# Softmax and feature steps of the first chunk moved between ScalarE, VectorE and GpSimd in a fused attention and feed-forward kernel

## The chip, the cores and the metric

The kernel runs on one core of a Trainium2 chip. A core has five engines that each work through their own queue in order: PE (TensorE, matmuls), DVE (VectorE), ACT (ScalarE), POOL (GpSimd) and SP, which here only issues DMAs. They wait for each other through semaphores. The metric is the device time of one execution in microseconds; lower is better. The kernel before took 885.22 us in the median of three runs (881.85 to 885.75).

## What is computed

The reference is attention with sparse masks on 8 sequences of 576 positions, 8 heads of width 64, followed by a feed-forward layer on the 4608 tokens:

```python
scores = scale * np.matmul(q, k.transpose(0, 1, 3, 2))
rel = pos[:, None] - pos[None, :]
mask_local = (rel >= 0) & (rel < stride)                        # heads 0 to 3, stride 32
mask_strided = (rel >= 0) & (pos[None, :] % stride == pos[:, None] % stride)   # heads 4 to 7
scores = np.where(masks, scores, -1e9)
attn = np.exp(scores - max); attn = attn / (sum + 1e-9)
x = matmul(attn, v) regrouped to (4608, 512)
h = np.maximum(x @ w_in, 0.0)          # w_in: 512 x 2048
out = h * h @ w_out                    # w_out: 2048 x 512
```

All of it is in fp32 accuracy: on PE each fp32 operand of the feed-forward layer is split into a high and a low part, and a product is three matmuls (high by high, low by high, high by low).

## The kernel before, in words

The 4608 tokens go in 12 chunks of 384. A chunk first needs its attention output x (written xlh, xll for the local heads and xsh, xsl for the strided heads, high and low part). Then `up` (L452) makes for each of 16 slices j of the hidden width twelve 128x384 matmuls into one of three PSUM banks (h), squares the positive part and splits it into gh and gl. `down` (L480) multiplies gh and gl by a slice of w_out, nine 128x512 matmuls, into three accumulator banks (y). While PE does the ups and downs of one chunk, the other engines make the attention of the next one.

The first chunk has nothing to hide behind, so all its heads run on PE in pairs (`pe_pair`, L292): `first` are the two pairs of local heads, `late` the two pairs of strided ones. A pair has these steps: scores on PE (L319); mask and minimum on DVE (L324); exponentials with their sum on ACT, one instruction per block (L345, `single`, the local pairs), or a subtraction on POOL (L347), one exponential per head on ACT (L348) and a sum on DVE (L349) (the others); the reciprocal of the sum on DVE (L350, L351); the division on POOL (L353), in SBUF; a transpose on PE (L359) and a copy out of PSUM on ACT (L360); the product with v on PE (L367, L378); high part on ACT (L382) and low part on DVE (L383).

Beside it `convert` (L147) unpacks the weights, which arrive as 1 MB tiles of 64-bit floats, in halves of 512: one scaling of the tile on ACT (L154), then for each half a step on ACT into PSUM (z, L166), one on DVE (L169), the high part on ACT (L172) and the low part on POOL (L173). `behind(..)` lets such work be issued only after a named instruction. In the prologue (L588 to L627) the order in which `next(..)` steps the pairs and the weights is the order in which they are handed to the scheduler, which then places each engine's queue; in the first chunk each up and down (L632 to L636) hands in two weight halves, behind the gh of that step (L652, L653), and a share of the next chunk's heads (L661 to L681). `zeros` (L583) issues matmuls on zeros whose result nobody reads: 60 at the start, 30 after the scores of the local pairs and 30 after those of the first strided pair.

In the first chunk `up` squares with ACT and DVE (L470, L471: ACT writes relu(h) to SBUF, DVE multiplies it with max(h, 0) in PSUM), ACT writes gh (L475) and DVE gl (L476); in the others ACT does both (L473, L474).

Of the kernel before, what the change touches and what calls it, by code (L numbers as in the profile page):

```python
# [22 lines left out]
P = 128  # L23
# [63 lines left out]
def attn_moe(ctx: ExitStack, tc, qk_l, v_l, qk_d, v_d, qk_p, v_p, f_s, q_s, k_s, v_s, w_in, w_out, masks, eye, out):  # L87
# [59 lines left out]
    def convert():  # L147

        split = None

        def scale(k):
            for raw, _ in raws[k]:

                nc.scalar.activation(f32(raw[:, :, 1]), f32(raw[:, :, 1]), AF.Prelu, scale=2.0**-112, alpha=-(2.0**32))  # L154

        scale(0)
        for k in range(NFT):
            p, which = order[k]
            t = wpool.tile([P, 2, 1024], F32R, name=f"w{which}_{p}", tag=f"w{k}")
            (wo if which else wi)[p] = t[:, 0], t[:, 1]  # L160
            cuts = [(raw[:, i : i + WP], sl.start + i) for raw, sl in raws.pop(k) for i in range(0, sl.stop - sl.start, WP)]
            for raw, at in cuts:

                z = psum(zbank[next(zturn) % len(zbank)], f"z{k}_{at}").bitcast(U32)
                w, hi, lo = raw[:, :, 1], t[:, 0, at : at + WP], t[:, 1, at : at + WP]
                first_step = nc.scalar.activation(z, raw[:, :, 0], AF.Copy, bias=-0.49, scale=2.0**-29 * (1 - 2.0**-9))  # L166
                if split:
                    split()
                last["v"] = nc.vector.scalar_tensor_tensor(out=w, in0=w, scalar=3, in1=z, op0=ALU.logical_shift_left, op1=ALU.bitwise_or)  # L169

                def split(w=w, hi=hi, lo=lo, at=at, k=k):
                    last["a"] = nc.scalar.copy(hi, f32(w))  # L172
                    last["g"] = nc.gpsimd.tensor_sub(lo, f32(w), f32(hi))  # L173
                    if at and 4 <= k < 12:
                        fetch(k + 4)

                if not at and k + 1 < NFT and k + 1 in raws:
                    with tc.issue_after(first_step.ins):
                        scale(k + 1)
                yield  # L180
        split()
# [110 lines left out]
    def pe_pair(c, pr, local, qk, vr, es, pt, banks, sm, single):  # L292


        u = f"{c}_{pr}_{int(local)}"
        if local:
            kw, wins, nv = KW, [at for _, _, at in windows(c)], P
            src, vsrc = qk_d[c, pr], v_d[c, pr]
            mk = [mask_sb[:QC, w % 2, :] for w in range(NW)]
        else:  # L300
            kw, wins, nv = QC, [QC * w for w in range(NW)], QC
            src, vsrc = qk_p[pr], v_p[pr]
            mk = [mask_sb[:QC, 3, :QC]] * NW
        nk = wins[-1] + kw
        nc.sync.dma_start(out=qk[:, : TC + nk], in_=src[:, : TC + nk])
        if c == 0:
            yield
        last["s"] = nc.sync.dma_start(out=vr[:nv], in_=vsrc)
        yield
        v4 = vr.rearrange("p (h w d) -> p h w d", h=2, w=NW)  # L310
        nm = small.tile([P, 2, NW], F32, name=f"nm{u}", tag="nm")
        rs = small.tile([P, 2, NW], F32, name=f"rs{u}", tag="rs")
        ss = sums[sm]

        s_ps = [banks() for _ in range(2)] if c == 0 else None
        e4 = [e[:QC, : NW * kw].rearrange("p (w k) -> p w k", k=kw) for e in es]
        def scores(h, w, s):
            rows = slice(D * h, D * (h + 1))
            last["p"] = nc.tensor.matmul(s[:QC, w * kw : (w + 1) * kw], qk[rows, w * QC : (w + 1) * QC], qk[rows, TC + wins[w] : TC + wins[w] + kw], start=True, stop=True)  # L319

        def minima(h, s):

            for w in range(NW):
                nc.vector.tensor_tensor_reduce(  # L324
                    out=e4[h][:, w], in0=s[:QC, w * kw : (w + 1) * kw], in1=mk[w], scale=-SCALE, scalar=3.0e38,
                    op0=ALU.add, op1=ALU.min, accum_out=nm[:QC, h, w : w + 1],
                )

        if s_ps:
            for w in range(NW):  # L330
                for h in range(2):
                    scores(h, w, s_ps[h])
            for h in range(2):
                minima(h, s_ps[h])
        else:
            for h in range(2):
                s = banks()
                for w in range(NW):
                    scores(h, w, s)
                minima(h, s)  # L340
        yield
        for h in range(2):
            if single:
                for w in range(NW):
                    last["a"] = nc.scalar.activation(e4[h][:, w], e4[h][:, w], AF.Exp, bias=nm[:QC, h, w : w + 1], scale=-1.0, accum_out=ss[:QC, NW * h + w, :1])  # L345
            else:
                nc.gpsimd.tensor_sub(e4[h], e4[h], nm[:QC, h].unsqueeze(2).broadcast_to([QC, NW, kw]))  # L347
                last["a"] = nc.scalar.activation(e4[h], e4[h], AF.Exp, scale=-1.0)  # L348
                nc.vector.tensor_reduce(out=ss[:QC, NW * h : NW * (h + 1), 0], in_=e4[h], op=ALU.add, axis=AX.X)  # L349
        nc.vector.tensor_reduce(out=rs[:QC].rearrange("p h w -> p (h w)"), in_=ss[:QC], op=ALU.add, axis=AX.X)  # L350
        last["v"] = nc.vector.reciprocal(rs[:QC], rs[:QC])  # L351
        for h in range(2):
            last["g"] = nc.gpsimd.tensor_mul(e4[h], e4[h], rs[:QC, h].unsqueeze(2).broadcast_to([QC, NW, kw]))  # L353
        yield
        p4 = pt.rearrange("p (h w q) -> p h w q", h=2, w=NW)
        for h in range(2):
            t = s_ps[h] if s_ps else banks()
            for w in range(NW):
                nc.tensor.transpose(t[:kw, w * QC : (w + 1) * QC], e4[h][:, w], ident[:QC, :QC])  # L359
            last["a"] = nc.scalar.copy(pt[:kw, h * TC : (h + 1) * TC], t[:kw, :TC])  # L360
        yield
        x = x_tiles(c)
        if local:
            o = s_ps[0] if s_ps else banks()
            for w in range(NW):
                for h in range(2):
                    nc.tensor.matmul(o[D * h : D * (h + 1), w * QC : (w + 1) * QC], v4[:kw, h, w], p4[:kw, h, w], start=True, stop=True)  # L367
            outs = [(o[:, :TC], [x["l", s][:, pr, :] for s in "hl"])]
        else:

            r0 = D * pr
            outs = []
            for a in range(2):
                o = s_ps[a]
                for w in range(NW):
                    for h in range(2):
                        p0 = r0 + STR * h
                        nc.tensor.matmul(o[p0 : p0 + STR, w * QC : (w + 1) * QC], v4[:kw, h, w, STR * a : STR * (a + 1)], p4[:kw, h, w], start=True, stop=True)  # L378
                by_i = lambda t: t[r0 : r0 + D].rearrange("p (s i r) -> p s i r", s=2, r=STR)
                outs.append((o[r0 : r0 + D, :TC].rearrange("p (s r i) -> p s i r", s=2, i=SI), [by_i(x["s", s][:, a, :]) for s in "hl"]))  # L380
        for src, (xh, xl) in outs:
            last["a"] = nc.scalar.copy(xh, src)  # L382
            last["v"] = nc.vector.tensor_sub(xl, src, f32(xh))  # L383
        yield
# [67 lines left out]
    def up(c, j):  # L452
# [14 lines left out]
        if c == 0:  # L467

            r = p_t[j % 2].rearrange("p w q -> p (w q)")
            nc.scalar.activation(r, g, AF.Relu)  # L470
            nc.vector.scalar_tensor_tensor(out=g, in0=g, scalar=0.0, in1=r, op0=ALU.max, op1=ALU.mult)  # L471
        else:
            nc.scalar.activation(g, g, AF.Relu)  # L473
            nc.scalar.activation(g, g, AF.Square)  # L474
        last["gh"] = nc.scalar.copy(gh, g)  # L475
        nc.vector.tensor_sub(gl, g, f32(gh))  # L476
        g_tiles[c, j] = gh, gl
        return done
# [122 lines left out]
    next(first[0])  # L601
    next(first[1])
    with tc.issue_after(last["p"].ins):
        zeros(0, NWARM // 2)
        for k in range(NEARLY, 8):
            fetch(k)
    next(late[0])
    with tc.issue_after(last["p"].ins):
        zeros(1, NWARM // 2)
    next(first[0])  # L610
    next(first[1])
    weights = behind({"a": last["a"]}, ungated)
    next(late[1])
    for i in range(2):
        next(first[0])
        next(first[1])
        next(late[0])
        next(late[1])
        if i:
            weights = behind({"a": last["a"]}, ungated)  # L620
        for _ in range(2):
            next(weights)
    next(late[0])
    next(late[1])
    for _ in range(2 * NEARLY - 4):
        next(weights)
    heads_end = {e: last[e] for e in "agsv"}  # L627
    zbank = (3, 4)
# [129 lines left out]
```

## Time and profile before

| | us |
|---|---|
| median of three runs | 885.22 |
| the profiled execution | 883.18 |
| its span in the trace | 881.4 |
| PE busy in the span | 868.5 (99%) |
| POOL busy | 676.8 (77%) |
| DVE busy | 635.5 (72%) |
| ACT busy | 572.6 (65%) |

The span is the time from the first to the last instruction in the trace; 1.8 us of the execution lie around it. Busy time of an engine is the time with an instruction of it in flight, so a PE that shows 100% has no gap, but says nothing of how fast its matmuls follow each other. The shares are means over stages: the first 30 us (the attention of the first chunk), the first chunk's ups and downs to about 105 us, and eleven chunks after that.

### The profile page before, as it was taken

The numbers are of one execution on the slowest core, as the hardware profiler recorded it, in microseconds if no ns is written. First come the engines' busy times: TensorE is split into PE (matmuls) and PEld (weight loads), VectorE is DVE, ScalarE is ACT, GpSimd is POOL, SyncE is SP. The second block draws the span as 40 slices with busy tenths as digits, with TensorE's granted clock in tenths as the row PEclk, the third lists the DMA queues.
The fourth block names the chain that finished last, engine by engine and source line by source line (L and its number), as shares of the span: only waits on it lengthen the run. The fifth ranks groups of instructions, "written<-read, shape, count | busy, mean of one in ns | idle before, by whom it ended". The sixth has DMA issues, their size and how long they took to land.

```text
span 881.4 us, 14862 instructions
## 1 busy us (share of the span) xinstructions
PE 868.5 (99%) x4744; PEld 789.6 (90%) x4744; DVE 635.5 (72%) x1892; ACT 572.6 (65%) x1510; POOL 676.8 (77%) x722
## 2 busy tenths in 40 slices
PE   8899999999999999999999999999999999999997
PEld 7788899999999999999999999999999989998996
DVE  4578687788777888878778778778787787883111
ACT  6798776676676666757657747657666665664332
POOL 4698878878978989898988978997898899782000
PEclk9999999999999999999999999999999999999999
DMA  9851631323123123104102302312131121000000
GB/s 356 355 195 63 184 121 42 103 84 113 32 66 112 37 89 103 44 30 127 44 13 80 115 14 74 104 31 74 31 102 57 30 71 61 7 1 10 28 1 36
DMA packets 26798, 71.41 MB, mean 81 GB/s; under 512 B 2976, under 2 KB 8736, under 8 KB 25184
## 3 DMA queue, kind: packets, MB, share of 16 engines
q1 hardware_dynamic: 26432, 70.14, 23.9%
q8 instruction: 37, 0.61, 0.3%
q10 hardware_dynamic: 288, 0.33, 0.1%
q14 instruction: 41, 0.34, 0.1%
HBM read 61.01 MB, written 9.44 MB: 80 GB/s over the span
## 4 chain that ended last, share of the span: by engine, by line
PE 95%; ACT 3%; DVE 1%; POOL 0%; issue 0%; DVEq 0%; POOLq 0%; ACTq 0%
PE h L462 44%; PE y L489 44%; PE s L234 2%; PE o L280 2%; ACT e L345 1%; PE w_ps L586 1%; ACT raw L154 1%; PE b L319 1%; DVE sc L419 0%; ACT z L166 0%; ACT w L172 0%; DVE raw L169 0%; ACT pt L360 0%; PE b L359 0%; DVE xsl L383 0%
## 5 line engine op out<-in xcount | busy, mean ns | idle before, releaser
L489 PE MATMUL y<-w,gh 128*128 128x512 f32 x1152 | 357.1, 391 | 0.8 <-ACT gh L475 0.8
L489 PEld LDWEIGHTS y<-w,gh 128*128 128x128 f32 x1152 | 212.5, 188 | 41.5 <-ACT gh L475 1.4
L462 PE MATMUL h<-xlh,w 128*128 128x384 f32 x768 | 229.6, 339 | 2.1 <-DVE xsl L383 1.6
L462 PE MATMUL h<-xsh,w 128*128 128x384 f32 x768 | 226.2, 335 | 0.0
L489 PE MATMUL y<-w,gl 128*128 128x512 f32 x576 | 224.0, 392 | 0.0
L434 POOL TENSOR_TENSOR pp<-vs,sc 128x448 f32<-128x448 f32 (+10 forms) x192 | 189.8, 1014 | 39.8 <-DVE qs L435 18.2
L412 POOL TENSOR_TENSOR pq<-ks,qs 128x512 f32<-128x512 f32 (+2 forms) x192 | 197.8, 1050 | 17.9 <-DVE sc L413 13.8
L476 DVE TENSOR_TENSOR gl<-h,gh 128x384 fp32r<-128x384 f32 x192 | 105.4, 550 | 84.2 <-ACT gh L475 82.9
L475 ACT CAST gh<-h 128x384 fp32r<-128x384 f32 x192 | 91.4, 477 | 103.0 <-PE y L489 100.0
L473 ACT ACTIVATE h<-h 128x384 f32<-128x384 f32 x176 | 83.0, 472 | 107.8 <-PE h L462 106.2
L413 DVE TENSOR_REDUCE sc<-pq 128x8 f32<-128x512 f32 (+4 forms) x228 | 119.6, 534 | 46.2 <-POOL pq L412 43.9
L462 PEld LDWEIGHTS h<-xlh,w 128*128 128x128 f32 x768 | 142.1, 188 | 5.6 <-DVE xsl L383 1.8
L462 PEld LDWEIGHTS h<-xsh,w 128*128 128x128 f32 x768 | 141.7, 188 | 0.3
L462 PE MATMUL h<-xll,w 128*128 128x384 f32 x384 | 129.3, 337 | 0.0
L435 DVE TENSOR_REDUCE qs<-pp 128x64 f32<-128x448 f32 (+11 forms) x192 | 106.7, 563 | 31.0 <-POOL pp L434 29.5
L489 PEld LDWEIGHTS y<-w,gl 128*128 128x128 f32 x576 | 108.1, 188 | 22.9
L462 PE MATMUL h<-xsl,w 128*128 128x384 f32 x384 | 128.5, 335 | 0.0
L474 ACT ACTIVATE h<-h 128x384 f32<-128x384 f32 x176 | 83.2, 473 | 3.6
L259 DVE STREAM_TRANSPOSE p_t<-e 32x128 f32<-32x128 f32 x240 | 72.3, 301 | 10.4 <-ACT e L248 6.0
L462 PEld LDWEIGHTS h<-xll,w 128*128 128x128 f32 x384 | 72.5, 189 | 2.2
L462 PEld LDWEIGHTS h<-xsl,w 128*128 128x128 f32 x384 | 72.2, 188 | 0.0
L243 ACT ACTIVATE e<-e,nm 96x128 f32<-96x128 f32 x160 | 62.5, 392 | 10.5 <-DVE nm L226 8.8
(97 smaller groups left out, 1077.2 us busy)
## 6 DMA issues: line engine op xcount, KB each, us to landing
qk<-qk_l SPq DMA_DIRECT2D x24, 400.0 KB, 3.2
y<-ysb SPq DMA_DIRECT2D x36, 256.0 KB, 3.7
raw<-w_in SPq DMA_DIRECT2D x7, 1024.0 KB, 11.2
qk<-qk_l SPq DMA_DIRECT2D x16, 416.0 KB, 3.3
vs<-v_s SPq DMA_DIRECT2D x10, 576.0 KB, 4.0
raw<-w_out SPq DMA_DIRECT2D x5, 1024.0 KB, 12.9
v<-v_l SPq DMA_DIRECT2D x40, 128.0 KB, 2.0
ks<-k_s SPq DMA_DIRECT2D x8, 576.0 KB, 3.8
```

The lines of the kernel that those rows point to most:

```text
L243: nc.scalar.activation(e[:QC, cut(w)], e[:QC, cut(w)], AF.Exp, bias=nmax[:QC, w : w + 1], scale=-1.0, accum_out=ssum[:QC, w, :1])
L259: nc.vector.transpose(out=pt[STR * k : STR * (k + 1), :, STR * r : STR * (r + 1)], in_=e.rearrange("p (w k) -> p w k", k=KW)[STR * r : STR ...
L412: nc.gpsimd.tensor_mul(pv, kt[:, a : a + m, :], qt[:, i - i0 : i - i0 + 1, :].broadcast_to([P, m, D]))
L413: nc.vector.tensor_reduce(out=sc[:, i - i0, a : a + m], in_=pv, op=ALU.add, axis=AX.X)
L434: nc.gpsimd.tensor_mul(pv, vt[:, a : a + nd, :n], sc[:, il : il + 1, :n].broadcast_to([P, nd, n]))
L435: nc.vector.tensor_reduce(out=ot[:, il, a : a + nd], in_=pv, op=ALU.add, axis=AX.X)
L462: done = nc.tensor.matmul(ph[:, :TC], w[:, wsl], xx, start=n == 0, stop=n == 11)
L473: nc.scalar.activation(g, g, AF.Relu)
L474: nc.scalar.activation(g, g, AF.Square)
L475: last["gh"] = nc.scalar.copy(gh, g)
L476: nc.vector.tensor_sub(gl, g, f32(gh))
L489: done = nc.tensor.matmul(y_ps[c][t], g[:, sl], w[:, wsl], start=j == 0 and k == 0, stop=j == NFT - 1 and k == 2)
```

## The change

It touches the first chunk alone, in seven places:

- Local pairs: the exponentials (L345 before, L352 now) are written to the PSUM bank of the scores instead of to SBUF, and the division (L353 before, L361 now) is made by DVE from that bank into SBUF instead of by POOL in SBUF.
- Strided pairs: the copy of the transposed exponentials out of PSUM (L360 before, L368 now) is made by DVE instead of ACT.
- Weights: the second half of the first tile is split into high and low part at once and not with the step after it; the prologue hands in the first tile's two halves ahead of the last steps of the local pairs, and the others after all steps of the pairs.
- The two groups of 30 matmuls on zeros are gone; 12 stand in their place, after the scores of all pairs, in unused columns of a strided pair's bank.
- The scores of the second strided pair are handed in directly behind those of the first.
- `up`: gh is written by DVE (L481), with the same instruction that then writes the square into PSUM; ACT's write of gh is gone for the first chunk, and ACT's relu stands there twice (L478, L479). What waits for gh's write on ACT (the weights) now waits for the second relu.
- What the scheduler makes of it is a new order on every engine of the first chunk.

```diff
@@ convert
+                if k == 0 and at:
+                    split()
+                    split = None
@@ pe_pair
+        r4 = [blocks(t) for t in s_ps] if single else e4
...
+            last["free"] = s_ps[0][:, TC : TC + P]
...
-                    last["a"] = nc.scalar.activation(e4[h][:, w], e4[h][:, w], AF.Exp, bias=nm[:QC, h, w : w + 1], scale=-1.0, accum_out=ss[:QC, NW * h + w, :1])
+                    last["a"] = nc.scalar.activation(r4[h][:, w], e4[h][:, w], AF.Exp, bias=nm[:QC, h, w : w + 1], scale=-1.0, accum_out=ss[:QC, NW * h + w, :1])
...
-            last["g"] = nc.gpsimd.tensor_mul(e4[h], e4[h], rs[:QC, h].unsqueeze(2).broadcast_to([QC, NW, kw]))
+            eng, key = (nc.vector, "v") if single else (nc.gpsimd, "g")
+            last[key] = eng.tensor_mul(e4[h], r4[h], rs[:QC, h].unsqueeze(2).broadcast_to([QC, NW, kw]))
...
-            last["a"] = nc.scalar.copy(pt[:kw, h * TC : (h + 1) * TC], t[:kw, :TC])
+            (nc.vector.tensor_copy if c == 0 and not local else nc.scalar.copy)(pt[:kw, h * TC : (h + 1) * TC], t[:kw, :TC])
@@ up
             nc.scalar.activation(r, g, AF.Relu)
-            nc.vector.scalar_tensor_tensor(out=g, in0=g, scalar=0.0, in1=r, op0=ALU.max, op1=ALU.mult)
+            last["gh"] = nc.scalar.activation(r, g, AF.Relu)
+            for t in (gh, g):
+                nc.vector.scalar_tensor_tensor(out=t, in0=g, scalar=0.0, in1=r, op0=ALU.max, op1=ALU.mult)
         else:
...
-        last["gh"] = nc.scalar.copy(gh, g)
+            last["gh"] = nc.scalar.copy(gh, g)
@@ the prologue, from the scores of the local pairs on
     with tc.issue_after(last["p"].ins):
-        zeros(0, NWARM // 2)
         for k in range(NEARLY, 8):
             fetch(k)
     next(late[0])
-    with tc.issue_after(last["p"].ins):
-        zeros(1, NWARM // 2)
+    next(late[1])
+
+    for _ in range(NWARM // 5):
+        nc.tensor.matmul(last["free"], warm, warm, start=True, stop=True)
+    next(first[0])
+    with tc.issue_after(last["a"].ins):
+        next(first[1])
+    weights = behind({"a": last["a"]}, ungated)
     next(first[0])
     next(first[1])
-    weights = behind({"a": last["a"]}, ungated)
+    next(late[0])
     next(late[1])
-    for i in range(2):
-        next(first[0])
-        next(first[1])
+    for _ in range(2):
+        next(weights)
+    next(first[0])
+    next(first[1])
+    for _ in range(2):
         next(late[0])
         next(late[1])
-        if i:
-            weights = behind({"a": last["a"]}, ungated)
-        for _ in range(2):
-            next(weights)
-    next(late[0])
-    next(late[1])
-    for _ in range(2 * NEARLY - 4):
+    weights = behind({"a": last["a"]}, ungated)
+    for _ in range(2 * NEARLY - 2):
         next(weights)
```

The order on three engines shows what this moves. ACT, at the end of the prologue, before (xsh: high part of the strided heads' output; z, w, raw: steps of the weights; raw_192 and raw_194 are the second and third tile):

```order
L360 COPY w_1_0_104<-b_1_0_355 96x384
L166 ACTIVATE z_0_468<-raw_192 128x512
L172 CAST w_0_413<-raw_190 128x512
L154 ACTIVATE raw_194<-raw_194 128x1024
L382 CAST xsh_425<-b_0_0_280 64x384
L382 CAST xsh_425<-b_1_0_354 64x384
L382 CAST xsh_425<-b_1_0_355 64x384
```

The same place now:

```order
L172 CAST w_0_363<-raw_190 128x512
L390 CAST xlh_375<-b_0_1_198 128x384
L390 CAST xlh_375<-b_1_1_218 128x384
L390 CAST xsh_377<-b_0_0_248 64x384
L390 CAST xsh_377<-b_0_0_249 64x384
L390 CAST xsh_377<-b_1_0_268 64x384
L390 CAST xsh_377<-b_1_0_269 64x384
L166 ACTIVATE z_0_460<-raw_192 128x512
L154 ACTIVATE raw_194<-raw_194 128x1024
```

The steps of the second and third tile now stand behind all of ACT's casts of the first chunk's x, and the copies of the strided pairs are gone from this queue. DVE, the same place before (xll, xsl: low parts of x; sums and rs: sums of the exponentials and their reciprocals):

```order
L349 TENSOR_REDUCE sums_94<-w_1_0_104 96x4
L350 TENSOR_REDUCE rs_1_0_353<-sums_94 96x8
L351 RECIPROCAL rs_1_0_353<-rs_1_0_353 96x8
L383 TENSOR_TENSOR xll_424<-b_1_1_218,xlh_423 128x384
L383 TENSOR_TENSOR xsl_426<-b_0_0_279,xsh_425 64x384
L169 SCALAR_TENSOR_TENSOR raw_192<-raw_192,z_0_468 128x512
L383 TENSOR_TENSOR xsl_426<-b_0_0_280,xsh_425 64x384
```

And now:

```order
L361 TENSOR_TENSOR e_1_1_114<-b_1_1_218,rs_1_1_217 96x512
L361 TENSOR_TENSOR e_1_1_115<-b_1_1_219,rs_1_1_217 96x512
L356 TENSOR_REDUCE sums_94<-w_1_0_104 96x4
L357 TENSOR_REDUCE rs_1_0_267<-sums_94 96x8
L169 SCALAR_TENSOR_TENSOR raw_190<-raw_190,z_0_364 128x512
L358 RECIPROCAL rs_1_0_267<-rs_1_0_267 96x8
L368 COPY pt_0_0_103<-b_0_0_248 96x384
L169 SCALAR_TENSOR_TENSOR raw_190<-raw_190,z_512_368 128x512
L368 COPY pt_0_0_103<-b_0_0_249 96x384
L391 TENSOR_TENSOR xll_376<-b_0_1_198,xlh_375 128x384
L368 COPY w_1_0_104<-b_1_0_268 96x384
L368 COPY w_1_0_104<-b_1_0_269 96x384
```

Divisions and copies are now in DVE's queue ahead of the low parts of x. POOL, at the end of the first chunk, before (pp: products of the strided heads of the second chunk; xsl_904: the last part of the second chunk's x; pq_4, kx, qx, vx: first work for the third chunk):

```order
L434 TENSOR_TENSOR pp_3_5_0_1183<-qkvs_3_973,sc_3_975 128x384
L173 TENSOR_TENSOR w_6_1218<-raw_0_1025,w_6_1218 128x512
L173 TENSOR_TENSOR w_6_1218<-raw_512_1027,w_6_1218 128x512
L446 TENSOR_TENSOR xsl_904<-qkvs_3_973,xsh_903 128x2x192
L173 TENSOR_TENSOR w_7_1271<-raw_0_1097,w_7_1271 128x512
```

And now (xsl_861 is that part):

```order
L442 TENSOR_TENSOR pp_3_5_0_1144<-qkvs_3_931,sc_3_933 128x384
L173 TENSOR_TENSOR w_7_1234<-raw_0_1057,w_7_1234 128x512
L221 TENSOR_TENSOR kx_0_1327<-qk_0_1316,kx_0_1327 128x448
L223 TENSOR_TENSOR qx_0_1326<-qk_0_1316,qx_0_1326 64x384
L258 TENSOR_TENSOR vx_0_1568<-v_0_1317,vx_0_1568 128x4x64
L420 TENSOR_TENSOR pq_4_0_0_1462<-qkvs_4_1458 128x64
L412 MEMSET sc_4_1460 128x108
L173 TENSOR_TENSOR w_7_1234<-raw_512_1059,w_7_1234 128x512
L420 TENSOR_TENSOR pq_4_1_0_1465<-qkvs_4_1458 128x128
L454 TENSOR_TENSOR xsl_861<-qkvs_3_931,xsh_860 128x2x192
```

The last part of the second chunk's x has moved from behind two instructions to behind eight, five of them for the third chunk.

## Rows read from the trace of the kernel before

**Rows 1.** Busy time by stretch; columns are named in the first line.

```profile
core 0: us, PE busy (x) PEld busy (x) DVE busy (x) ACT busy (x) POOL busy (x), PEclk, DMA share, GB/s
0.00:30.00 30.00, 23.53 (x312) 20.48 (x312) 13.32 (x83) 20.35 (x59) 14.19 (x24) 1.00 0.95 372
30.00:35.00 5.00, 4.56 (x18) 4.56 (x19) 2.80 (x5) 4.69 (x9) 2.64 (x2) 0.66 1.01 405
200.00:300.00 100.00, 100.00 (x528) 91.48 (x527) 79.50 (x249) 66.59 (x186) 85.91 (x99) 1.00 0.26 78
...
40.00:100.00 60.00, 59.52 (x337) 51.82 (x336) 48.03 (x126) 53.28 (x99) 51.90 (x53) 1.00 0.39 138
```

**Rows 2.** The chain of waits in the first 45 us: start, us, what.

```profile
8.76 6.27 ACT e L345 x32
...
27.27 0.54 ACT z L166
...
28.41 1.05 ACT raw L154
29.46 0.36 ACT xsh L382
```

**Rows 3.** PE in order of time: start, us, engine, line, what [idle before <-releaser].

```profile
30.44 0.69 PE L462 MATMUL h<-xlh,w 128*128 128x384 f32 x1 [1.61 <-DVE xsl L383]
...
39.17 1.66 PE L489 MATMUL y<-w,gh 128*128 128x512 f32 x6 [0.79 <-ACT gh L475]
40.66 0.85 PE L489 MATMUL y<-w,gl 128*128 128x512 f32 x3
...
106.38 0.33 PE L462 MATMUL h<-xsl,w 128*128 128x384 f32 x1
```

**Rows 4.** DVE in order of time, in the prologue.

```profile
8.36 0.29 DVE L324 CUSTOM_DVE_ANT_0 e<-b,mask_sb 96x128 f32<-96x128 f32 x1 [8.36 <-PE b L319]
...
8.58 0.28 DVE L324 CUSTOM_DVE_ANT_0 e<-b,mask_sb 96x128 f32<-96x128 f32 x1
...
18.19 0.54 DVE L349 TENSOR_REDUCE sums<-e 96x4 f32<-96x384 f32 x1
...
18.65 0.70 DVE L169 SCALAR_TENSOR_TENSOR raw<-raw,z 128x512 uint32<-128x512 uint32 x1
```

**Rows 5.** DVE's groups of instructions, 38 to 100 us: busy us, mean ns.

```profile
L169 DVE SCALAR_TENSOR_TENSOR raw<-raw,z 128x512 uint32<-128x512 uint32 x24 | 16.4, 683 | 4.3 <-ACT z L166 3.9
L471 DVE SCALAR_TENSOR_TENSOR h<-h,p_t 128x384 f32<-128x384 f32 x14 | 7.8, 561 | 3.8 <-ACT p_t L470 3.8
```

**Rows 6.** The line of the output copies, 100 to 200 us: ns min/median/max.

```profile
L493 DVE COPY ysb<-y x4: 676/678/692, 113.8 to 184.6; 128x512 f32<-128x512 f32 x4
```

**Rows 7.** Busy time by microsecond, the columns of rows 1.

```profile
16.00:17.00 1.00, 0.29 (x4) 0.13 (x3) 0.45 (x1) 1.00 (x4) 1.00 (x3) 1.00 1.06 442
...
29.00:30.00 1.00, 0.00 (x0) 0.00 (x0) 0.16 (x1) 0.97 (x3) 0.79 (x1) 1.00 1.07 447
```

**Rows 8.** DVE and POOL side by side at 80 us, in order of time.

```profile
79.16 5.15 POOL L173 TENSOR_TENSOR w<-raw,w 128x512 fp32r<-128x512 f32 x4
...
80.47 3.89 DVE L419 TENSOR_TENSOR sc<-sc,mx 128x36 f32<-128x36 f32 x1
```

**Rows 9.** POOL in order of time, at the end of the first chunk.

```profile
98.98 1.31 POOL L173 TENSOR_TENSOR w<-raw,w 128x512 fp32r<-128x512 f32 x1 [1.55 <-ACT w L172]
101.51 1.33 POOL L173 TENSOR_TENSOR w<-raw,w 128x512 fp32r<-128x512 f32 x1 [1.22 <-ACT w L172]
102.86 1.02 POOL L446 TENSOR_TENSOR xsl<-qkvs,xsh 128x384 fp32r<-128x384 f32 x1
...
106.07 1.16 POOL L218 TENSOR_TENSOR kx<-qk,kx 128x448 fp32r<-128x448 f32 x1
107.31 1.01 POOL L220 TENSOR_TENSOR qx<-qk,qx 64x384 fp32r<-64x384 f32 x1
108.88 0.73 POOL L255 TENSOR_TENSOR vx<-v,vx 128x256 fp32r<-128x256 f32 x1
```

More of the change, by code (lines that the diff above doesn't have):

```diff
@@ L315, in pe_pair @@
         s_ps = [banks() for _ in range(2)] if c == 0 else None
-        e4 = [e[:QC, : NW * kw].rearrange("p (w k) -> p w k", k=kw) for e in es]
+        blocks = lambda t: t[:QC, : NW * kw].rearrange("p (w k) -> p w k", k=kw)
+        e4 = [blocks(e) for e in es]
+        r4 = [blocks(t) for t in s_ps] if single else e4
         def scores(h, w, s):
```

## Prediction

> **What bounds the kernel now.** I read the busy time by stretch first. From 200 to 300 us PE is busy in all 100.00 us, and in the first chunk, from 40 to 100, in 59.52 of 60 [rows 1]. So the time is the moment at which PE starts its first `up`, plus the gaps after it, plus the time that matmuls spend at the lower clock. PE in order of time gives the first two: the first `up` starts at 30.44, released by a low part (xsl) from DVE, and the first `down` at 39.17, after 0.79 us of waiting for gh from ACT [rows 3]. For the clock, 30:35 shows 0.66 of full speed, a mixture of the two levels of 1.2 and 2.4 GHz [rows 1]; it follows a microsecond in which PE did nothing, at clock 1.00 [rows 7]. With 4.56 us of PE in that stretch, about 4.56 x 0.34 = 1.5 us is lost there.
>
> What makes the first `up` so late is told by the chain of waits: it runs down ACT's queue, from the exponentials at 8.76 over a weight step (z, 0.54) and a scaling of a whole tile (raw, 1.05) to the strided high parts at 29.46 [rows 2]. DVE is busy in only 13.32 of the first 30 us, ACT in 20.35 [rows 1]. Up to 30 us ACT is the bound and DVE has room; from 40 to 100 us the three helpers are loaded alike (48.03, 53.28 and 51.90 of 60).
>
> **The change part by part.** *ACT's front.* Gone from ahead of the last high part: z 0.54 and raw 1.05, which stand behind it now, and four copies. A copy is taken at the 0.36 of a cast of the same width [rows 2]: 4 x 0.36 = 1.4. Together 3.0, so by ACT alone the first `up` would start at 30.44 - 3.0 = 27.4.
>
> *DVE's front.* Of the 13.32 us that DVE worked before 30 us one weight step (0.70) [rows 4] now comes later: 12.6. Added are four divisions of 96x512 and four copies of 96x384. No row shows a division out of PSUM. Below it lies the 0.54 of a reduce over 384 [rows 4], above it the 0.68 of an output copy out of PSUM over 512 [rows 6] and the same of a weight step [rows 5]; following instructions start 0.46 apart where one lasts 0.54 [rows 4], so I take 0.60. A copy is the output copy's 0.68 x 384/512 = 0.51. Sum 12.6 + 4 x 0.60 + 4 x 0.51 = 17.1, which from the first mask at 8.36 [rows 4] ends at 25.4 if DVE never waits. It will wait now and then for exponentials, transposes and high parts. The two ends are thus 25.4 and, by ACT with a little waiting left, 27.9; I take 26.9, near ACT's end, since each low part still needs ACT's high part first. The first `up` gains 3.5 (2.5 to 5.0).
>
> The division reads the exponentials from PSUM and only the reciprocals from SBUF. With two inputs in SBUF, an instruction of DVE (L419) took 3.89 us beside four subtractions of POOL that took 5.15 [rows 8]. The Trainium skill, "SBUF — State Buffer", section "Who interferes with whom", says that a DVE instruction with at most one SBUF input, outside the two-port modes, does not contend with GpSimd; by that rule the divisions keep the 0.60. Were they held like L419, by one subtraction of about 5.15/4 = 1.3 each, the front would lose up to 4 x 1.3 = 5.2 and the 3.5 would become a loss of 1.7. I leave the 0.60, and the rest of the sum needs no more than that.
>
> *Masks, fewer zeros, the order of the scores.* 0.22 us a block on DVE [rows 4], as before; the zeros are not waited for by anyone, so I cost them at nothing unless the clock falls (rival C).
>
> *The first `down`.* Behind its last high part ACT has three z, two casts and two raws before its first relu; with a cast taken like z that is 5 x 0.54 + 2 x 1.05 = 4.8. Then two relus, z, a cast and the second relu. From a last high part at about 26.5 this puts the second relu at about 34 and DVE's gh at about 35. PE itself, at the same pace as before (39.17 - 0.79 - 30.44 = 7.9 for the first ups), would be ready at 26.9 + 7.9 = 34.8. So the wait for gh stays, of some 0.4 in place of 0.79, and `down` starts near 35.2. gl now stands on DVE behind gh, the square, a weight step and the next two of `up`, 2.2 us more, so the third part of `down` starts near 37.4 against 40.66 [rows 3]: 3.2 ahead. Since PE has no gaps afterwards, I take **3.1** as what the front brings (2.0 to 4.6, with the spread of the first `up`).
>
> *DVE's extra instruction.* One more per `up`, nearest row 0.56 for the square itself [rows 5], some 0.48 where it follows directly: 14 x 0.48 = 6.7 in this stretch, so DVE goes from 48.03 to about 54.7 of 60. ACT's relu is there twice, each about as long as the cast of gh that goes, so ACT wins nothing. That is hidden as long as DVE delivers gl in time; cover left, 5 of 60 us.
>
> *The end of the first chunk.* The last low part of the second chunk's x was on POOL from 102.86 to 103.88 [rows 9], and PE first read it at 106.38 [rows 3]: 2.5 us of room. PE will want it 3.1 us sooner, at 103.3. In POOL's queue kx, qx, vx and first products of the third chunk now stand ahead of it: 1.16 + 1.01 + 0.73 [rows 9] plus about 1.0 for two products and a memset, 3.9 in all. POOL had waits of 1.55 and 1.22 for ACT's casts ahead of it [rows 9], 2.8 that this work may fill. If POOL's clock of work does not move, the part ends at 103.88 + 3.9 = 107.8 without any filling and at 105.0 with all of it: PE would wait 1.7 to 4.5. If POOL too runs 3.1 ahead, it ends 101.9 to 104.7, and PE waits 0 to 1.4. POOL was busy in 51.90 of 60 [rows 1], so it can follow only in part: I take **2.5** (0 to 4.5).
>
> Sum: 883.18 - 3.1 + 2.5 = 882.6 for an execution like the profiled one. The three runs have a mean of 884.3, 1.1 above it, and a median of 885.22, 2.0 above. With the first, 883.7; I forecast **883.8**.
>
> **The rivals.** *A: the front's gain is kept.* The waits in POOL's queue are filled and it follows PE's head start; then 883.18 - 3.1 + 1.1 = 881.2, and 879.7 if the 1.5 us of low clock also goes, since PE's last waits before the first `up` may be shorter. For it: every engine had gaps at 40 to 100 us [rows 1], and 2.8 us of them stand directly ahead of the moved work [rows 9]. Against: POOL's and DVE's share.
>
> *B: POOL's low part comes much later (slower).* The strided heads of the second chunk are made by DVE and POOL in turn, and DVE has 6.7 us more to do there, with instructions that POOL can hold for 3.89 [rows 8]. If the part of POOL ends at 110, PE waits 110 - 103.3 = 6.7, and the sum is 883.18 - 3.1 + 6.7 + 1.1 = 887.9. It decides from the point at which the part ends after 103.3 + 3.1 = 106.4; up to there the front pays for the wait. For it: the order puts eight instructions ahead where there were two. Against: what POOL does ahead of it must be done anyway, and its inputs may be ready early.
>
> *C: the low clock spreads over the prologue (slower).* At 16:17 PE was busy in 0.29 at clock 1.00, and two groups of 30 matmuls on zeros stood before that; now 12 stand there. If PE falls to 1.2 GHz there, its steps from 16 to 26.9 take twice as long: at 0.29 busy, 0.29 x 10.9 = 3.2 us more, most of it on the path, while the 1.5 at the first ups is as before. Then 883.18 - 3.1 + 3.0 + 2.5 + 1.1 = 886.7. For it: in 30:35, after an idle microsecond, the clock was 0.66 [rows 1, 7]. Against: sparse work kept it at 1.00. The Trainium skill, "TensorE: Matmul & The Clock Gate", section "What's actually happening", has the throttled state as the default that activity releases; by that the missing zeros speak for C, while the full clock at 0.29 busy does not bear it out.
>
> **How the numbers follow.** Forecast (the gain is given back at the second chunk) 0.41, 883.8, own range 882.3 to 886.2; A 0.29, 881.2 down to 879.7; B 0.19, 887.9 and up to 890.5 with the division held or a still later part; C 0.11, 886.7. The range from 879.8 to 888.4 leaves out the lowest part of A and the upper half of B. About 0.5% is what a measurement of this kernel can tell from no change: below 880.8 is faster, above 889.6 slower. Faster takes half of A and a little of the forecast, 0.19; slower takes a part of B and the tail of C, 0.11; the rest, 0.70, is the same.
>
> **What would show it.** Right: the first `up` between 26 and 27.9, released by DVE; the first `down` near 35 and its third part near 37.4; divisions of 0.55 to 0.70; DVE some 54 to 55 of 60 us busy; a wait of PE of some 2 us at the second chunk's first `up`, for POOL's low part. No such wait would mean A; one of more than 3.1, B. A clock under 1.00 between 12 and 26 us would mean C. The prediction is wrong in its first step if the first `up` starts after 28.5, and in its last if PE waits in the ups in between, for gl or gh, since I put no cost there.

## The result and the profile after

The changed kernel takes 886.01 us in the median of 20 runs (885.1 to 887.87), the kernel before 884.47 in as many (881.85 to 886.27). The ratio is 1.0022, with a 95% interval of 1.0015 to 1.0029: 0.2% slower, 1.5 us between the medians and 1.9 between the means. The forecast was 883.8, a little below the kernel before. The runs of the changed kernel lie in two groups, 885.1 to 886.2 with a mean clock of 0.989 to 0.991, and 886.9 to 887.9 with 0.987 or 0.988, and the profiled one (887.28, span 885.5) is of the second, so that the two profiled executions lie 4.1 us apart and the medians only 1.5.

Busy time by stretch, with the columns of [rows 1] (PEclk is the clock granted to PE, as a share of 2.4 GHz), tells most of it:

```profile
0.00:30.00 30.00, 23.27 (x226) 19.97 (x228) 16.12 (x88) 16.80 (x51) 10.20 (x20) 0.72 0.96 376
30.00:35.00 5.00, 4.85 (x60) 4.64 (x57) 3.31 (x6) 4.30 (x8) 0.00 (x0) 0.96 1.02 405
40.00:100.00 60.00, 59.44 (x316) 52.20 (x317) 51.99 (x142) 55.46 (x101) 53.59 (x57) 0.97 0.41 137
200.00:300.00 100.00, 100.00 (x527) 91.39 (x526) 79.60 (x251) 66.71 (x188) 83.51 (x97) 1.00 0.26 77
```

The clock of the first 30 us is 0.72, where it was 1.00 [rows 1]. Finer cuts of the same view show when it falls:

```profile
10.00:11.00 1.00, 0.69 (x18) 0.62 (x15) 1.00 (x11) 0.97 (x6) 0.00 (x0) 1.00 1.02 385
12.00:13.00 1.00, 0.00 (x0) 0.00 (x0) 1.00 (x13) 0.97 (x6) 0.26 (x1) 1.00 1.02 410
13.00:14.00 1.00, 0.00 (x0) 0.00 (x0) 1.00 (x14) 1.00 (x6) 1.00 (x2) 0.65 0.95 385
20.00:30.00 10.00, 10.00 (x78) 7.72 (x78) 4.72 (x9) 4.92 (x10) 4.19 (x4) 0.50 1.00 418
```

PE has nothing to do after 10.69, and between 13 and 14 us its clock falls to the lower level of 1.2 GHz. From 20 to 30 us it is busy all the time at 0.50: PE is now the bound of the prologue, and ACT and DVE wait for it. PE in order of time, as in [rows 3]:

```profile
14.22 1.44 PE L620 MATMUL b<-p_t 128*128 128x128 bf16 x12 [3.53 <-DVE nm L330]
...
18.82 0.87 PE L367 MATMUL b<-ident,e 96*128 96x96 f32 x4 [1.07 <-ACT w L355]
...
31.86 0.44 PE L470 MATMUL h<-xlh,w 128*128 128x384 f32 x1
...
40.56 2.90 PE L499 MATMUL y<-w,gh 128*128 128x512 f32 x6 [1.68 <-DVE gh L481]
43.26 1.22 PE L499 MATMUL y<-w,gl 128*128 128x512 f32 x3
...
108.09 0.95 PE L470 MATMUL h<-xlh,w 128*128 128x384 f32 x2 [0.58 <-ACT xlh L390]
111.38 0.45 PE L470 MATMUL h<-xsl,w 128*128 128x384 f32 x1 [0.54 <-POOL xsl L454]
```

The 12 matmuls on zeros (L620) wait 3.53 us for DVE's minima. The first `up` starts at 31.86 against 30.44, the first `down` at 40.56 against 39.17 after a longer wait for gh (1.68 against 0.79), and its first six matmuls take 2.90 against 1.66 [rows 3]: a second stretch at the lower clock, with 0.58 on average from 40 to 44 us. At the second chunk two waits of 1.12 us in all are new, one of them for POOL's low part. That closes the account of the two profiles: counted from the first mask, the third part of the first `down` (gl) starts 2.5 us later, it takes 0.4 more itself, and the second chunk adds 1.1, together 4.0 of the 4.1.

The first exponential also starts later. ACT's first, after DVE's first mask at 8.49, and DVE's divisions:

```profile
9.52 0.37 ACT L352 ACTIVATE b<-e,nm 96x128 f32<-96x128 f32 x1 [6.84 <-DVE nm L330]
```
```profile
15.44 1.27 DVE L361 TENSOR_TENSOR e<-b,rs 96x512 f32<-96x512 f32 x2
```

From the first mask to the first exponential it is 1.03 us, where it was 8.76 - 8.36 = 0.40 [rows 2, 4].

### The profile page after: what moved, and what is told of

Same layout as the page of the kernel before. It is cut to its first block, busy times and chain, and to the rows that moved or that the text cites. A ratio compares the mean times of both kernels' runs of the same rounds, so it can differ in the third digit from the quotient of the medians.

```text
span 885.5 us, 14782 instructions
## 1 busy us (share of the span) xinstructions
PE 870.5 (98%) x4696; PEld 790.2 (89%) x4696; DVE 645.0 (73%) x1916; ACT 571.6 (65%) x1506; POOL 672.8 (76%) x718
## 4 chain that ended last, share of the span: by engine, by line
PE 95%; DVE 1%; ACT 1%; POOL 1%; issue 0%; DVEq 0%; POOLq 0%
PE y L499 44%; PE h L470 44%; PE s L237 2%; PE o L283 2%; PE w_ps L596 1%; PE b L367 1%; PE b L325 1%; PE b L375 1%; DVE e L330 0%; ACT raw L154 0%; PE b L386 0%; ACT z L166 0%; POOL w L173 0%; POOL pp L442 0%; DVE raw L169 0%
## 5 line engine op out<-in xcount | busy, mean ns | idle before, releaser
L485 ACT CAST gh<-h 128x384 fp32r<-128x384 f32 x176 | 83.6, 476 | 98.5 <-PE y L499 97.6
L443 DVE TENSOR_REDUCE qs<-pp 128x64 f32<-128x448 f32 (+11 forms) x192 | 106.6, 563 | 32.4 <-POOL pp L442 30.7
```

What stands on the lines that cost most here:

```text
L443: nc.vector.tensor_reduce(out=ot[:, il, a : a + nd], in_=pv, op=ALU.add, axis=AX.X)
```

## The experiments

A label's ratio is to the kernel before, run beside it on the same chip in three sets (its median there 883.9 to 884.2). "Low part" is POOL's xsl, the last part of the second chunk's x.

| label | against the changed kernel | median us | ratio [95%] |
|---|---|---|---|
| e1_zeros_back | both zero groups back | 888.37 | 1.0049 [1.0031, 1.0068] |
| e5_zeros_30_12 | zero groups of 30 and 12 back | 890.50 | 1.0070 [1.0049, 1.0091] |
| e7_xsl_first | POOL's low part first | 885.45 | 1.0014 [1.0005, 1.0023] |
| e6_zeros_xsl_first | both zero groups back and low part first | 881.97 | 0.9974 [0.9965, 0.9983] |
| e4_one_relu | one relu per up | 890.21 | 1.0075 [1.0059, 1.0091] |
| e8_zeros_xsl_one_relu | e6 and one relu | 885.54 | 1.0023 [1.0012, 1.0034] |
| e9_zeros_xsl_gh_act | e6 and gh by ACT | 880.77 | 0.9966 [0.9954, 0.9979] |
| e11_best_divide_pool | e9, division on POOL | 882.98 | 0.9995 [0.9985, 1.0004] |
| e12_best_copies_act | e9, strided copies on ACT | 880.36 | 0.9960 [0.9948, 0.9972] |
| e13_best_no_12 | e9 without the 12 zeros | 880.27 | 0.9963 [0.9949, 0.9977] |
| e2_before_no_zeros | (before) without its two groups | 885.99 | 1.0019 [1.0010, 1.0028] |
| e10_before_xsl_first | (before) low part first | 883.74 | 1.0000 [0.9991, 1.0009] |

The scheduler places all queues anew for each, so an edit at one place also moves some instructions elsewhere. Since the start of a run shifts (DVE's first mask comes at 7.49 to 8.97 us), moments are compared from DVE's first mask on: before, the first `up` comes 22.1 us after it and the third part of the first `down` (gl) 32.3; in the changed kernel 23.4 and 34.8.

**The zeros.**

```diff
     with tc.issue_after(last["p"].ins):
+        zeros(0, 30)
         for k in range(NEARLY, 8):
             fetch(k)
     next(late[0])
+    with tc.issue_after(last["p"].ins):
+        zeros(1, 30)
     next(late[1])
```

> The changed kernel with the two groups of 30 matmuls on zeros put back where they were (one after the scores of the local pairs, one after those of the first strided pair); the 12 of the change stay. Theory 1 (the clock): in the changed kernel PE stood still from 10.69 to 14.22 us and its clock was half from 13.4 to 30.4, so that transposes and products with v took twice as long and PE itself held the first up back; with the groups back the clock is 1.00 from 12 to 26 us, the first up starts between 26.5 and 29 instead of 31.86, and the time falls by 2.5 to 5 us against the changed kernel, to 881 to 883.5. Theory 2 (the new queues of DVE and ACT are the bound, the clock only fills what would be waiting): the first up stays at 31 or later and the time within 1 us of the changed kernel.

The clock is 1.00 from 10 to 40 us and the first `up` comes 20.6 us after the first mask, its `down`'s third part 31.3: 2.8 and 3.5 sooner than in the changed kernel, 1.5 and 1.0 sooner than before. The moment is the one theory 1 gave, but the time went up. The busy time by stretch and PE show where:

```profile
100.00:110.00 10.00, 6.67 (x42) 5.07 (x42) 5.61 (x14) 4.12 (x10) 9.37 (x14) 0.92 0.56 161
110.00:120.00 10.00, 10.00 (x41) 9.07 (x40) 5.45 (x23) 6.41 (x20) 3.73 (x4) 0.74 0.48 173
```
```profile
109.46 0.69 PE L470 MATMUL h<-xsl,w 128*128 128x384 f32 x1 [3.03 <-POOL xsl L454]
```

PE waits 3.03 us for POOL's low part of the second chunk's x, and from within the wait on the clock is down: 0.74 over the next 10 us is 5.2 us at half speed, 2.6 lost. POOL ahead of it, in order of time:

```profile
97.74 0.96 POOL L442 TENSOR_TENSOR pp<-qkvs,sc 128x384 f32<-128x384 f32 x1
...
102.58 1.15 POOL L221 TENSOR_TENSOR kx<-qk,kx 128x448 fp32r<-128x448 f32 x1
103.81 1.01 POOL L223 TENSOR_TENSOR qx<-qk,qx 64x384 fp32r<-64x384 f32 x1
104.90 0.72 POOL L258 TENSOR_TENSOR vx<-v,vx 128x256 fp32r<-128x256 f32 x1
105.56 0.42 POOL L675 MEMSET p_t<- 128x384 f32 x1
105.94 1.28 POOL L420 TENSOR_TENSOR pq<-qkvs 128x192 f32<-128x192 f32 x2
107.17 1.29 POOL L173 TENSOR_TENSOR w<-raw,w 128x512 fp32r<-128x512 f32 x1
108.42 0.99 POOL L454 TENSOR_TENSOR xsl<-qkvs,xsh 128x384 fp32r<-128x384 f32 x1
```

From 102.58 on that is the third chunk's work and a weight, without a gap. In the changed kernel less stands there:

```profile
102.17 1.81 POOL L442 TENSOR_TENSOR pp<-qkvs,sc 128x320 f32<-128x320 f32 x2
...
110.32 1.01 POOL L454 TENSOR_TENSOR xsl<-qkvs,xsh 128x384 fp32r<-128x384 f32 x1
```

From the end of the last product (pp) to the low part it is 6.3 us there and 9.7 in e1: the zeros, put back, also moved POOL's queue. This second cause is tested with e6 and e7.

> As the kernel with both groups back, but only 12 in the second group, so that the scores of the second strided pair come about 1 us sooner and DVE's minima wait less. Theory 1: full clock as well, first up up to 1 us earlier than with 30 and 30, time 880.5 to 883; if 12 are too few and the clock falls to half before 16 us, the time is that of the changed kernel (885 to 887). Theory 2: no difference between the three.

Here (the second group with `zeros(1, 12)`) the clock did fall, to 0.65 from 20 to 30 us, and the first `up` came 23.6 after the first mask; a wait of 3.04 for POOL followed. Worse than expected on both counts. But with e1 it makes the cleanest pair on the clock: in both the first mask is at 8.23, and PE has the same 80 matmuls to do from the second to the third of these lines, in e1:

```profile
20.00:30.00 10.00, 8.30 (x110) 6.44 (x109) 7.55 (x18) 6.51 (x15) 5.68 (x6) 1.00 1.02 421
22.84 1.07 PE L367 MATMUL b<-ident,e 96*96 96x96 f32 x8
28.84 0.44 PE L470 MATMUL h<-xlh,w 128*128 128x384 f32 x1
```

and in e5:

```profile
20.00:30.00 10.00, 8.46 (x80) 6.48 (x80) 5.96 (x15) 4.93 (x10) 5.68 (x6) 0.65 1.01 419
22.90 1.66 PE L367 MATMUL b<-ident,e 96*96 96x96 f32 x8
31.87 0.69 PE L470 MATMUL h<-xlh,w 128*128 128x384 f32 x1
112.91 0.69 PE L470 MATMUL h<-xsl,w 128*128 128x384 f32 x1 [3.04 <-POOL xsl L454]
```

Up to 22.9 us the clock is 1.00 in both; then 6.0 us at full and 9.0 at half clock, so the 3.0 us are the clock's. And e5's front is as late as the changed kernel's (23.6 and 23.4), yet its wait for POOL is as long as e1's, so an early front is not what makes that wait long. Counted from the first `up`, POOL's part ends 1.1 (e1) and 1.5 us (e5) later than in the changed kernel, behind the longer queue (10.1 us from the last product in e5), and PE gets there 1.4 and 1.0 sooner, since it runs at full clock through its first `down`, where the changed kernel loses 1.6.

> The kernel before without its two groups of 30 matmuls on zeros, and nothing else changed. Theory 1: the clock falls to half between 12 and 15 us and stays there for most of the prologue; the transposes take 0.8 in place of 0.4 us, the first up starts 1.5 to 4 us later than 30.44, and the time is 886 to 889. Theory 2 (PE has slack in the prologue, since ACT is its bound): the first up within 0.5 us of 30.44 and the time within 1 us of before.

Its diff takes the two `zeros(..)` groups out of the kernel before. The clock falls (0.69 from 10 to 20, 0.62 from 20 to 30), PE idle for 6.28 us until 17.23; but the first `up` is not later (21.9 after the first mask). In the old order PE had room, and half speed used it up (busy 9.99 of 10 from 20 to 30); at the first `up` it still waits 0.64 for a weight from ACT. The loss, 0.19%, stands at the first `down`, which waits 2.36 us for gh, and at 40 to 50 us with a clock of 0.83; why gh comes later was not looked into. So my moment for the loss was wrong, its size at the low end of what I named.

**POOL's low part first.**

```diff
-            nc.gpsimd.tensor_sub(x["s", "l"][:, :, cols], src, f32(x["s", "h"][:, :, cols]))
+            last["xsl"] = nc.gpsimd.tensor_sub(x["s", "l"][:, :, cols], src, f32(x["s", "h"][:, :, cols]))
...
-        if j == NFT - 2:
+        if j == NFT - 2 and c:
             take(c + 2, "010")
...
                 run(st)
+                if c == 0:
+                    weights_end["x"] = last["xsl"]
+                    take(2, "010")
```

> The changed kernel with both groups of 30 matmuls on zeros back, and with all work for the third chunk handed in only after POOL's low part of the second chunk's strided x (kx, qx, vx, pq stand behind it on POOL). With the zeros alone PE waited 3.03 us for that part at 106.4 and then ran at a clock of 0.74 from 110 to 120 us, which is about 2.6 us more. Theory 1 (two causes: the clock in the prologue, and that part's place in POOL's queue): no wait of over 0.5 us and clock 1.00 from 100 to 120; the time falls by 4 to 6 us against the kernel with the zeros alone (888.4), to 882.5 to 884.5. Theory 2 (the helpers have too much work in the first chunk; the place in the queue only decides what is late): another wait of 1.5 us or more stands at 100 to 115 us, for ACT's or DVE's parts, and the time is 886 or more.

> The changed kernel, without zeros, with the third chunk's work behind POOL's low part of the second chunk's strided x. Theory 1: the waits of 0.58 and 0.54 at 108 to 112 us go, nothing else: 884.5 to 885.5, against 886.0. Theory 2: waits of the same size for other parts, time 886 within 0.7.

> The kernel before with nothing changed but that the third chunk's work is handed in behind POOL's low part of the second chunk's strided x. There that part already stood ahead of it (102.86 to 103.88, needed at 106.38, no wait). Theory 1: the same time as before within 0.8 us, so that the gain of the best version (880.8) is not this order by itself. Rival: the new order frees something else at the boundary, and the time falls by 1.5 us or more.

With the zeros and this order, no wait for POOL is left:

```profile
100.00:110.00 10.00, 9.77 (x61) 7.99 (x60) 5.83 (x16) 6.72 (x16) 7.97 (x12) 1.00 0.67 224
110.00:120.00 10.00, 10.00 (x53) 9.04 (x52) 8.66 (x33) 8.24 (x27) 6.88 (x8) 1.00 0.55 180
```

881.97 is 6.4 below the zeros alone (3.3 of waits and 2.6 of low clock make 5.9), and below the kernel before. Without the zeros the order brings 0.6: of the two waits of 1.1 us POOL's goes and ACT's 0.58 stays. In the kernel before it brings nothing. The four together are the evidence: the zeros alone cost 2.4 us, the order alone saves 0.6, both save 4.0. So the faster front pays only once the low part no longer stands behind the third chunk's work. Part of the 2.4 is the zeros' own effect on POOL's queue (9.7 us where it was 6.3).

**The relu and gh.** One relu: the second `nc.scalar.activation(r, g, AF.Relu)` in `up` is gone. gh by ACT:

```diff
-            last["gh"] = nc.scalar.activation(r, g, AF.Relu)
-            for t in (gh, g):
-                nc.vector.scalar_tensor_tensor(out=t, in0=g, scalar=0.0, in1=r, op0=ALU.max, op1=ALU.mult)
+            nc.vector.scalar_tensor_tensor(out=g, in0=g, scalar=0.0, in1=r, op0=ALU.max, op1=ALU.mult)
+            last["gh"] = nc.scalar.copy(gh, g)
```

> The changed kernel with ACT's relu once per up instead of twice; zeros as in the changed kernel. If ACT's queue is what the first down waits for, its wait of 1.68 us shrinks by 0.4 to 0.8, PE's second stretch at half clock (40.2 to 44 us) may go with it, and the time falls by 0.5 to 2.5 us, to 883.5 to 885.5; the first up stays at 31.5 to 32. If the gh on DVE's queue is what counts, the wait stays and the time is within 0.5 us of the changed kernel.

> As the kernel with the zeros and the low part first, and ACT's relu once per up. The changed kernel with one relu alone had taken 890.2 us, with waits of 4.1 us in all at 106 to 112 for ACT's and POOL's parts of the second chunk's x; its wait at the first down was 1.24 against 1.68. If the place of that work in the queues had cost it, this one shows no such wait, has the first down 0.4 to 1 us earlier than the kernel with two relus, and takes 881 to 883.5. If the load of DVE and POOL is the cause, it takes 886 or more.

> As the kernel with the zeros and the low part first, but gh is written by ACT after DVE's square, as before the change, so DVE has one instruction less per up and ACT's relu stands there once. If DVE's extra instruction is hidden, the time is within 1 us of the kernel with gh by DVE; if DVE's 52 of 60 busy us hold the second chunk's x back, it is 1.5 us or more below it; if the longer chain at the first down counts, that wait grows from 1.64 to over 2 and the time is 0.5 to 1.5 above.

One relu less made it slower, 890.21 alone and 885.54 on top of e6, against every expectation. The first `down` did come sooner after the ups (in e8 a wait of 0.89 instead of 1.64), but at the second chunk parts of x were late: in e8 waits of 0.7 for DVE, 0.6 and 0.6 for ACT and 0.5 for POOL, PE busy 7.57 of 10 from 100 to 110. There POOL's low part waits for ACT's high part, and that for DVE's transposes; the new order had put weights ahead of the products (pp) that DVE needs, and at two of them POOL waits 3.11 and 0.92 us for ACT, which itself waits up to 1.74 for a tile of w_out to arrive. What in the scheduler does that was not tried. gh by ACT brings DVE down from 53.14 to 46.13 busy us of 60 and the time from 881.97 to 880.77; the two intervals overlap, and the edit also shortens the wait at the first `down` (1.39 for 1.64). So DVE's extra instruction costs about a microsecond, if that: it was nearly hidden.

**The parts of the prologue**, each put back in e9:

```diff
-        r4 = [blocks(t) for t in s_ps] if single else e4
+        r4 = e4
...
-            eng, key = (nc.vector, "v") if single else (nc.gpsimd, "g")
+            eng, key = nc.gpsimd, "g"
```

> The best version so far (zeros back, low part first, gh by ACT; 880.8 us) with the exponentials of the local pairs in SBUF and their division on POOL again, as before the change. If the division on DVE shortens the chain to the first up, this one has its first up 0.5 to 2 us later than 29.6 and takes 881.3 to 883; if the later start of the exponentials (9.52 in place of 8.76, since they now write the bank that the masks read) eats that, the first up is within 0.4 us and the time within 0.5 us, or even lower.

In e12 the line of the copies is `last["a"] = nc.scalar.copy(pt[:kw, ...` for all pairs; in e13 the loop of the 12 is gone.

> The best version with the four copies of the strided pairs' transposes on ACT again. ACT is idle from 24.3 to 26.1 us in the version with DVE's copies and they stand between PE's steps, so which engine makes them should count little: first up within 0.4 us of 29.6 and the time within 0.6 us of 880.8. If ACT's queue is still the bound of the front, the first up is 1 us or more later and the time 1 us or more above.

> The best version without the 12 matmuls on zeros after the scores of all pairs; they stood on PE at 18.4 to 19.2 us, after 0.89 us of waiting for DVE's minima. If the two groups of 30 keep the clock by themselves, the clock stays 1.00 and PE's steps after it come up to 1 us sooner: time 880 to 881. If the clock needs them, it is 0.5 in some stretch from 16 to 33 us and the time is 1.5 to 4 us above 880.8.

With the division on POOL the time is 2.2 us up, as expected, but not by the way expected: the first `up` comes 18.6 after the first mask, 2.0 sooner, because it now stands ahead of the strided pair's last products although the clock is only 0.92 and 0.91 from 10 to 20 and from 20 to 30 us; after that PE waits 0.67 for a weight's low part from POOL, 1.06 for gh and 1.34 for gl, and the third part of the first `down` is at 33.5 against 30.7. So the first `up` alone is not the measure of the front. The copies' engine makes no difference (0.4 us). Without the 12 the clock falls in part (0.73 from 20 to 30 us) and the time is the same: its first `up` comes 20.5 us after the first mask, as with them. Half speed ended between 25 and 26 us (0.81 there), about where the last 64 products begin (25.58), and what it cost ahead of them was room that PE had (busy 9.18 of 10 from 20 to 30 us, where e9 has 8.29). In e5 it lasted beyond 32 us and covered them. e9, e12 and e13 are the best versions, 0.34 to 0.40% under the kernel before.

## Why the prediction was wrong

**The front's gain of 3.1 us** is the step that failed: it was a loss of 2.5 (third part of the first `down`, from the first mask on). Of these 5.6 us the clock has 3.5 (34.8 in the changed kernel against 31.3 with the zeros back and a clock of 1.00, e1), a part of it at the first `down` itself, and a front that is slower than forecast even at full clock has 2.1 (it gains 1.0 there, not 3.1). The clock's term had been put at nothing, with the sentence "the zeros are not waited for by anyone, so I cost them at nothing unless the clock falls (rival C)". The clock fell, to 0.50, and by the prediction's own signs (a first `up` after 28.5, a clock under 1.00 between 12 and 26 us) its first step was wrong. Rival C, given 0.11, is what happened, at 886.7 against a measured 886.0. That its number is so near is in part luck: it has the front at -0.1 us and the second chunk at 2.5, where the profile has a loss of 2.5 and a wait of 1.1. I had read 1.00 at 0.29 busy [rows 7] as evidence against it; but these rows come after dense work (PE was busy in all of 10 to 16 us), and the order showed that PE would have none at all between the scores and the minima, which the changed kernel has as 3.53 us. The Trainium skill, "TensorE: Matmul & The Clock Gate", section "What's actually happening", has activity as what keeps PE from its throttled default; the trace agrees (0.65 from 13 to 14 us, after PE had stood still since 10.69), and the rule should have weighed more than the row.

Rival C's working was off too: it took PE's busy share of 0.29 as what doubles. At half speed every step of PE in the chain is longer (26 products take 2.44 us in e5 and 1.34 in e1), and from 20 to 30 us PE was busy 10.00 of 10.

**Even at full clock the front gains 1.5 at the first `up`, not 3.5** (e1, e6: 20.6 against 22.1 from the first mask). Two things were missing; how the 2.0 us part between them is not shown. The exponentials write the bank that the masks read, so the first waits for the masks of a whole head: 0.63 us. With the exponentials in SBUF again (e11, first mask at 7.67) the first follows after 0.39:

```profile
8.06 0.40 ACT L352 ACTIVATE e<-e,nm 96x128 f32<-96x128 f32 x1 [5.38 <-DVE nm L330]
```

And sums by engine miss the alternation at the end; the chain of waits of e6 has it:

```profile
25.27 0.86 PE b L386 x15
26.15 0.48 ACT xsh L390
26.66 0.55 DVE xsl L391
27.21 0.47 DVE w L368
27.73 1.52 PE b L386 x30
29.27 0.47 ACT xsh L390
```

From 25.3 on each of PE, ACT and DVE waits for the one before it, whatever the sum of its queue, and the first `up` follows on PE's own last products at 29.16, with no wait for DVE, whom the forecast had as its releaser. DVE's sum ended at 25.4; it was used as a lower end, and the truth lay past the upper, 27.9 (20.6 after the first mask is 29.0 in the time of before).

**The first `down`.** I saw that the wait for gh would stay, at 0.4; it was 1.68 in the changed kernel and 1.64 in e6:

```profile
29.16 0.44 PE L470 MATMUL h<-xlh,w 128*128 128x384 f32 x1
...
38.03 1.63 PE L499 MATMUL y<-w,gh 128*128 128x512 f32 x6 [1.64 <-DVE gh L481]
```

From the first `up` to the first `down` it is 8.9 us there, where I had 35.2 - 26.9 = 8.3, so the chain over ACT was 0.6 too short; and at full clock PE was through its ups in 38.03 - 1.64 - 29.16 = 7.2, not 7.9.

**The end of the first chunk.** The mechanism (the third chunk's work ahead of POOL's low part holds PE up) was right, and e6 and e7, which take it away, show it; but in the changed kernel there was no gain of the front to give back. Its size went with POOL's queue and with PE's pace before it, and not with the moment of the first `up` (e5): 1.1 us of waits in the changed kernel, 0.54 of them for POOL, and 3.3 plus 2.6 of low clock in e1; I had 2.5 and no clock in it. Rival B put the stop at 6.7.

**Right:** DVE's division took 0.68 (0.60 taken, 0.55 to 0.70 named), its copies 0.55 (0.51). The first of the two divisions at 15.44 began while POOL subtracted (12.74 to 15.9), and two more ran beside POOL's own divisions:

```profile
17.98 1.28 DVE L361 TENSOR_TENSOR e<-b,rs 96x512 f32<-96x512 f32 x2
```
```profile
18.17 1.61 POOL L361 TENSOR_TENSOR e<-e,rs 96x384 f32<-96x384 f32 x2 [2.25 <-DVE rs L358]
```

All four took 0.676 to 0.686 us; the rule of "SBUF — State Buffer", section "Who interferes with whom", in the Trainium skill, held. DVE was busy 51.99 of 60, not the 54.7 of the forecast, and e9 shows that its extra instruction was nearly hidden.

## What to carry to other kernels

Work that nobody waits for can still carry something: before taking filler matmuls away, look in the order at how long TensorE then stands still, and price the steps of its chain that follow at half speed: here that cost the first `up` nothing where PE had room (e2, e13) and 3.0 us where it had none (e5). Where a stage is made earlier, follow the inputs of the next stage through the same queues; test the two together, because one alone showed a loss here (e1) and the other next to nothing (e7). And add up a chain along its hand-overs, not only engine by engine.

## What the runs showed that was not expected

- A wait costs more than itself. After PE's 3.03 us from 106.43 on (e1) its clock was 0.74 from 110 to 120 us, 2.6 us more; after the 1.68 at the first `down` the six matmuls took 2.90 in place of 1.66. After 1.63 to 1.65 us at the same place in e1, e5, e6 and e7 the clock stayed at 1.00; what decides is not settled.
- With the clock at half, the kernel before lost nothing at its first `up` (e2), the changed one 2.8 us (against e1), and e5 3.0: the price of a slow PE depends on whether it has room.
- Less work on ACT (one relu instead of two) took 3.6 to 4.2 us more (e8 to e6, e4 to the changed kernel). In e8's trace weights stand ahead of the products in POOL's queue and make x late; why the scheduler made that order is open.
